# Switch-routed experts after local attention: experts' rows read as whole regions and turned in 32x32 blocks

## The chip, the cores and the metric

One core of a Trainium2 chip runs the whole program. The metric is the device time of one execution in microseconds, the median over several runs. The engines are named as in the profile: PE (TensorE, matrix products), DVE (VectorE), ACT (ScalarE), POOL (GpSimd) and SP, which issues most transfers.

## What is computed

An attention block with 4 batches, 8 heads, 768 positions and heads of 64, and behind it a layer of 8 experts, of which each token takes one. Cut from the reference:

```python
scores = scale * q @ k.T                      # per batch and head
keep = is_global | is_local                   # the first 8 keys, and the last 96 up to the query
scores = where(keep, scores - slope[h] * dist, -1e9)
a = softmax(scores);  attn = a @ v
x = attn.transpose(0, 2, 1, 3).reshape(3072, 512)
logits = x @ w_gate                           # 512 x 8
expert_idx = argmax(logits); gate_w = softmax(logits)[expert_idx]
for e in range(8):
    xe = x[expert_idx == e]
    out[expert_idx == e] = gate_w * (relu(xe @ w1[e]) @ w2[e])   # 512 x 1024, 1024 x 512
```

All data is float32.

## The kernel before

The program is recorded as one list of operations (`Flow`), and each engine runs its own operations in the order of that list; waits are derived from what each operation reads and writes. So the place of a line in the list is its place in its engine's queue, and an operation that waits holds up whatever stands behind it on the same engine. A transfer belongs to the queue of the engine that issues it: SP for plain loads, POOL for gathers and scatters.

**Attention** runs in 24 steps of 128 tokens (`steps(n)`, six per batch). A step computes the scores of its own block against itself and the block before (L456), adds the distance terms on DVE (`weigh`, L466, in two halves), takes the exponential on ACT (L474), sums on POOL (`both`, L480), and multiplies with the values of the step before (`values_part`, L493). It also finishes older blocks: `sums` and `tokens_x` (L508, L515) transpose the finished output, `tokens_u` (L518) the small sums, `normal` (L527 to L531) makes logits, `rows` (L536) writes the token's row. `k_in` (L432) and `q_in` (L440) transpose the keys and queries of two steps ahead. `k_in` uses a PSUM bank that the second half of `weigh` reads; `tokens_x` writes the bank that `rows` reads. POOL copies the global keys and values over the first rows of a block (L980, L1025). SP issues the loads of q and k four steps ahead, of v three steps ahead, and from step 5 on one piece of expert 0's weights per step.

**Routing.** After every sixth block `choose` finds each token's expert, `counts` ranks the tokens with small products on PE, `slots` turns ranks into row numbers, and six `scatter` calls per batch write rows of 516 words (512 of x, the gate, the token's number) into a table in device memory, xg_dram, where every expert has a region of its own. The ninth region (E, "late") takes expert 0's tokens of the last batch, so that expert 0 can start on the first three batches. `tables` and `all_counts` make the lists by which rows are gathered, the masks of unused rows, and the index of the size form of each group.

**Experts** run in the order 0, E, 1 to 7. `gather` (L702, on POOL) reads a group's rows, 128 per call. `x_in` transposes them on PE, four 128x128 transposes per 128 rows (L725), and ACT evicts them (L727). The two products of an expert are each done with seven products of quarter matrices instead of eight (`seven`): `up` twice seven steps (steps 0 to 13), `down` seven (steps 14 to 20; D is 14). All products stand in L758. Sums of quarters come from DVE: `x_sums` (L732 to L735), `w_sums` (L662 to L665, 128x1024 elements each), `h_sums` (L819 to L822), and inside the steps the additions that evict PSUM (L784, L795, L799, L804, L809); ACT copies the first product of each seven out (L780). `at_(i, ...)` hangs other work behind step i. `y_out` transposes the results back (L741), scales them by the gate (L744) and scatters them to the output (L747, POOL). `marks` copies the gates and makes the output row numbers from the gathered rows. `w_pieces(e)` are the eight weight transfers of an expert, 512 KB each, on SP. Group E uses plain products (`plain`).

At a boundary between two experts the order before is:

```python
ex.marks(g)
for j in (1, 3, 0, 2):
    ex.x_in(g, j)
if nxt is not None and g != E:
    ex.gather(nxt, [])
for fn in ex.x_sums():
    fn()
```

and then the first two up steps with the results of the group before between them.

## Time and profile before

| | |
|---|---|
| three runs | 572.89 us median, 572.22 to 573.99 |
| the profiled execution | 570.95 us, of which the span from first to last instruction is 569.2 |
| PE busy | 502.5 us, 88% of the span |
| DVE, ACT, POOL busy | 333.4 us (59%), 193.2 us (34%), 175.6 us (31%) |
| mean granted PE clock | 0.964 |
| the quarter products (L758) | 314.8 us of PE |
| transposes of x (L725) and of y (L741) | 19.4 us and 18.8 us of PE, 136 each |
| moved by DMA | 72.76 MB, mean 128 GB/s |

How to read it: a group of instructions is named by its line, engine and operation. The clock row gives, for each fortieth of the span, the share of full speed that PE was granted. A list of waits names for each engine what ended its idle time. In a timeline row the columns are the start and length in us, the engine (PEld are weight loads, an engine with a q at its end is its queue), the line, the operation, what it writes and reads, how many instructions the row covers, and in brackets the idle time before it and what ended that. Ends of matmuls are modelled.

### The profile page before, as it was taken

To read this page: it belongs to the slowest core of one execution; us is meant where nothing else is said; L and a number is where in the kernel's file an instruction comes from. 1 tells how busy PE (TensorE), PEld (TensorE's weight loads), DVE (VectorE), ACT (ScalarE), POOL (GpSimd) and SP (SyncE) were. 2 spreads that over 40 slices of the span, in tenths; PEclk is the share of its full clock that TensorE was granted. 3 is DMA by queue.
4 is the path that set the end of the run, shared out by engine and by line. 5 is a ranking of instruction groups with operands and counts; after the bars stand their busy time and mean duration, and the time that the engine had idled before them with its cause. 6 is when DMAs were issued, how large, how long until landed. Compare 5 with 4: busy or idle time off the path is not lost.

```text
span 569.2 us, 11005 instructions
## 1 busy us (share of the span) xinstructions
PE 502.5 (88%) x4537; PEld 468.8 (82%) x4537; DVE 333.4 (59%) x596; ACT 193.2 (34%) x325; POOL 175.6 (31%) x205
## 2 busy tenths in 40 slices
PE   4999899898774979989999999999999999999940
PEld 4888788787654879979998998999999998998940
DVE  5465855887762662716674674665774664666520
ACT  3666465566232220332223223223223213205200
POOL 2654475676454044322005014005005005003020
PEclk9999999999796989989999999999999999999995
DMA  8978787574152055371443433443443433001010
GB/s 180 216 190 213 202 218 202 137 185 122 40 170 85 1 184 190 126 260 33 149 150 119 149 150 106 149 150 118 149 150 112 149 116 134 1 1 60 1 40 7
DMA packets 97547, 72.76 MB, mean 128 GB/s; under 512 B 80568, under 2 KB 80568, under 8 KB 97472
## 3 DMA queue, kind: packets, MB, share of 16 engines
q1 hardware_dynamic: 89280, 52.70, 31.9%
q0 software_dynamic: 7360, 18.99, 9.8%
q8 instruction: 54, 0.88, 0.6%
q14 instruction: 21, 0.17, 0.1%
q10 hardware_dynamic: 832, 0.02, 0.1%
HBM read 61.69 MB, written 15.25 MB: 135 GB/s over the span
## 4 chain that ended last, share of the span: by engine, by line
PE 75%; DVE 11%; issue 4%; ACT 3%; POOL 2%; DMA 2%; POOLq 0%; ACTq 0%; DVEq 0%; SPq 0%
PE psum L758 50%; PE psum L456 6%; PE psum L493 5%; DVE arena L466 4%; PE psum L741 3%; PE psum L432 2%; PE psum L508 2%; PE psum L725 2%; PE psum L440 2%; PE psum L515 2%; ACT arena L727 2%; DVE arena L822 1%; DMA xg_dram<-arena,slot_i 1%; DVE arena L784 1%; DMA words<-in_n_local_dram 1%
## 5 line engine op out<-in xcount | busy, mean ns | idle before, releaser
L758 PE MATMUL psum<-arena 128*128 128x208 f32 (+6 forms) x1920 | 314.8, 325 | 9.6 <-DVE arena L784 5.5
L758 PEld LDWEIGHTS psum<-arena 128*128 128x128 f32 x1920 | 303.3, 191 | 17.1 <-DVE arena L784 7.6
L702 POOL DMA_INDIRECT arena<-xg_dram,grow x34 | 37.1, 1092 | 204.9 <-DVE arena L732 169.2
L466 DVE TENSOR_TENSOR arena<-psum,arena 128x1024 f32<-128x1024 f32 x40 | 48.7, 1220 | 39.1 <-PE psum L456 39.1
L480 POOL TENSOR_TENSOR arena<-arena 128x512 f32<-128x512 f32 x40 | 54.0, 1350 | 36.5 <-ACT arena L474 36.4
L474 ACT ACTIVATE arena<-arena 128x1024 f32<-128x1024 f32 (+1 forms) x48 | 47.4, 987 | 52.5 <-DVE arena L466 48.5
L747 POOL DMA_INDIRECT out_dram<-arena,to x34 | 35.4, 1040 | 75.2 <-ACT arena L744 39.7
L776 ACT ACTIVATE arena<-arena 128x512 f32<-128x512 f32 x48 | 30.2, 630 | 76.7 <-DVE arena L799 41.4
L493 PE MATMUL psum<-arena 128*64 128x128 f32 x704 | 45.6, 282 | 7.7 <-POOL arena L1025 6.6
L456 PE MATMUL psum<-arena 64*128 64x128 f32 x704 | 48.5, 288 | 1.4 <-ACT arena L434 0.7
L493 PEld LDWEIGHTS psum<-arena 128*64 128x64 f32 x704 | 39.3, 140 | 11.1 <-POOL arena L1025 7.0
L456 PEld LDWEIGHTS psum<-arena 64*128 64x128 f32 x704 | 43.6, 196 | 5.5 <-issue 3.2
L727 ACT COPY arena<-psum 128x512 f32<-128x512 f32 x34 | 18.5, 588 | 78.9 <-PE psum L725 78.9
L795 DVE TENSOR_TENSOR arena<-arena,psum 128x512 f32<-128x512 f32 x24 | 16.5, 688 | 45.8 <-PE psum L758 40.4
L588 POOL DMA_INDIRECT xg_dram<-arena,slot_i x24 | 24.1, 1002 | 28.4 <-DVE grow L687 23.5
L784 DVE TENSOR_TENSOR arena<-arena,psum 128x512 f32<-128x512 f32 x24 | 16.5, 686 | 27.6 <-PE psum L758 27.6
L432 PE MATMUL psum<-ident,arena 128*128 128x128 f32 x96 | 16.9, 303 | 15.3 <-DVE arena L466 8.6
L809 DVE TENSOR_TENSOR arena<-arena,psum 128x512 f32<-128x512 f32 x24 | 16.5, 688 | 21.9 <-PE psum L758 20.4
L799 DVE TENSOR_TENSOR arena<-arena,psum 128x512 f32<-128x512 f32 x24 | 16.5, 687 | 19.1 <-PE psum L758 17.1
L432 PEld LDWEIGHTS psum<-ident,arena 128*128 128x128 f32 x96 | 11.1, 151 | 19.9 <-issue 13.2
L804 DVE TENSOR_TENSOR arena<-arena,psum 128x512 f32<-128x512 f32 x24 | 16.5, 688 | 16.0 <-PE psum L758 13.4
L744 ACT ACTIVATE arena<-psum,gate 128x512 f32<-128x512 f32 x32 | 20.4, 684 | 11.0 <-PE psum L741 10.8
(137 smaller groups left out, 516.2 us busy)
## 6 DMA issues: line engine op xcount, KB each, us to landing
arena<-in_moe_w_dram SPq DMA_DIRECT2D x64, 512.0 KB, 4.3
arena<-in_q_dram SPq DMA_DIRECT2D x24, 256.0 KB, 3.9
arena<-in_k_dram SPq DMA_DIRECT2D x24, 256.0 KB, 4.6
arena<-in_v_dram SPq DMA_DIRECT2D x24, 256.0 KB, 5.1
arena<-xg_dram,grow POOLq DMA_INDIRECT x34
out_dram<-arena,to POOLq DMA_INDIRECT x34
xg_dram<-arena,slot_i POOLq DMA_INDIRECT x24
arena<-in_v_dram SPq DMA_DIRECT2D x4, 64.0 KB, 3.5
```

The source lines that it names most:

```text
L432: f.pe.transpose(pt[:, m, :], raw[:, 2 * m:2 * m + 2, :].rearrange("p a d -> p (a d)"), self.keep["ident"][:])
L456: f.pe.matmul(self.psum[:, 2 * g + a, c:c + P], lhsT=kt[r, m, :], rhs=qt[r, m, :], start=True, stop=True, skip_group_check=True)
L466: f.dve.tensor_tensor(e, s, self.bias[:, g, :, 1:3, :].rearrange("p h k c -> p h (k c)"), ALU.add)
L474: f.act.activation(e, e, AF.Exp)
L480: f.pool.tensor_tensor(self.es[n % 3][:, g], e[:, :, 0:P], e[:, :, P:2 * P], ALU.add)
L493: f.pe.matmul(po[r, m, :], lhsT=self.v[(n - ab) % 6][:, 2 * m + a, :], rhs=self.e[n % 2][:, m // 2, 2 * a + m % 2, P * ab:P * ab + P], sta ...
L588: self.f.pool.indirect_dma_start(out=self.xs[:], out_offset=bass.IndirectOffsetOnAxis(ap=k["slot_i"][:, b % 2, u:u + 1], axis=0), in_=self ...
L702: self.f.pool.indirect_dma_start(out=self.x[g][:, j, :].bitcast(I32), out_offset=None, in_=self.xs[:], in_offset=bass.IndirectOffsetOnAxis ...
L727: f.act.copy(self.xt[:, :, hh, ts(bb, 128)], pt)
L747: f.pool.indirect_dma_start(out=self.out[:], out_offset=bass.IndirectOffsetOnAxis(ap=k["to"][:, g, j:j + 1], axis=0), in_=self.y[j], in_of ...
L758: f.pe.matmul(self.psum[:, bank, 256 * t:256 * t + 256], lhsT=w[k][:, ts(t, 128)], rhs=x[k], start=(fresh and t == 0 and k == 0), stop=Tru ...
L776: f.act.activation(d, d, act)
```

## The change

- The gathers are gone. `load_x` reads a group's region as a whole with plain transfers on SP: four per half of the rows, each of 32 partitions x 8 runs of 512 bytes, and one or two small ones of 8 bytes per row for gate and token number (into `gt`). They are laid out so that a transpose within blocks of 32x32 gives the layout that the products read.
- `x_in` is now two DVE block transposes per expert (one for E), 128x1024 elements each, without PE, PSUM and ACT. To fit the order of channels that this gives, the w1 pieces take their rows in another order: 4 blocks of 32 rows for each piece.
- Rows of a region that no token fills have to be zero. `blank` writes zeros over the regions of 0, 1 and E after step 1 of attention (SP, 1280 rows of 2064 bytes); `pads` scatters zeros to the unused rows of experts 2 to 7 (POOL, four calls per expert), by `pad_table`.
- For experts 1 to 7 the first two of each four `w_sums` are on POOL.
- The order is new: in a step, `counts` one step later, `slots` behind the second half of `weigh`, `q_in` ahead of `k_in` and both behind `tokens_x`; the last batch's six scatters of step 21 in one go; the routing of the last batch spread over steps 2 to 14 of group 0; x work of the next expert at the down steps; `h_sums` spread over steps 7 to 13 instead of behind steps 6 and 13.

The core of the diff:

```diff
+    def gates(self, b):          # split off from choose()
+        f, k, V = self.f, self.keep, self.f.dve
...
-        x, xl = a(4, self.XW), a(2, self.XW)
+        x, xl = a(2, 8, 4, 32), a(1, 8, 4, 32)
...
+        s = self.moe_w1[e].rearrange("(q c d) f -> c q d f", q=4, d=32)
+        for c in range(4):
+            out.append(lambda d=w["w1"][:, c, :], s=s[c]: f.sp.dma_start(out=d, in_=s))
...
-        return [lambda: V.tensor_tensor(c["t3"], c["b22"], c["b12"], ALU.subtract),
-                lambda: V.tensor_tensor(c["t1"], c["b12"], c["b11"], ALU.subtract),
+        first = self.f.pool if e else V
+        return [lambda: first.tensor_tensor(c["t3"], c["b22"], c["b12"], ALU.subtract),
+                lambda: first.tensor_tensor(c["t1"], c["b12"], c["b11"], ALU.subtract),
...
+    def load_x(self, g, tokens):
+        f, k = self.f, self.keep
+        late = g == self.E
+        nh = 1 if late else 2
+        rows = self.xs[g * self.REGION:g * self.REGION + 256 * nh, :]
+        for hh in range(nh):
+            for qd in range(4):
+                src = rows[:, ts(qd, 128)].rearrange("(b t h) d -> h t b d", t=32, h=nh)[hh]
+                f.sp.dma_start(out=self.x[g][32 * qd:32 * qd + 32, hh].rearrange("p b c d -> p b (c d)").bitcast(I32),
+                               in_=src, _r=list(tokens))
...
-    def x_in(self, g, j, bank=None):
-        f = self.f
-        pt = self.bank() if bank is None else self.psum[:, bank, :].rearrange("p (c t) -> p c t", c=4)
-        for c in range(4):
-            f.pe.transpose(pt[:, c, :], self.x[g][:, j, ts(c, 128)], self.keep["ident"][:])
-        hh, bb = (j % 2, j // 2) if g != self.E else (0, j)
-        f.act.copy(self.xt[:, :, hh, ts(bb, 128)], pt)
+    def x_in(self, g, hh):
+        self.f.dve.transpose(out=self.xt[:, :, hh, :].rearrange("p c (b t) -> p b c t", t=32),
+                             in_=self.x[g][:, hh])
...
-            if n == N - 1:
-                ex.gather(0, sum(tokens[:B - 1], []))
...
-                kk = at.k_in(n + 2, SK)
             if n >= 2:
                 at.tokens_x(n - 2, T0)
             if n + 2 < N:
                 qq = at.q_in(n + 2, T1)
+                kk = at.k_in(n + 2, SK)
...
+                f.pool.memset(ex.zero, 0.0)
+                for g in (0, 1, E):
+                    ex.blank(g)
...
-            for _ in range(3 if b == B - 1 and i >= 3 else 1):
+            for _ in range(NBLK if b == B - 1 and i >= 3 else 1):
                 if scat:
                     at.scatter(*scat.pop(0))
+            if n == N - 3:
+                ex.load_x(0, sum(tokens[:B - 1], []))
...
+                if nxt is not None and g != E:
+                    ex.load_x(nxt, [f"pad{nxt}.{j}" for j in range(4)])
...
+                h0, h1 = ex.h_sums(0), ex.h_sums(1)
+                for i, fn in zip((7, 8, 9, 11), h0):
+                    at_(i, fn)
+                at_(13, *h1)
...
+                    last = sum(tokens, [])
+                    ex.load_x(E, last)
+                    for fn in pieces[:4]:
+                        fn()
+                    ex.load_x(1, last)
+                at_(2, lambda: at.normal(N - 1, U), lambda: at.choose(B - 1), *pieces[4:])
+                at_(4, lambda: at.counts(U), lambda: at.gates(B - 1))
+                at_(5, lambda: at.slots(B - 1, U))
+                at_(6, lambda: at.rows(N - 1, T0), scatters)
...
+                at_(0, sums[0], sums[1], sums[4], sums[5])      # group E: POOL's four for expert 1
+                at_(2, sums[2])
+                at_(3, sums[3], lambda: ex.x_in(1, 0))
+                at_(4, lambda: ex.x_in(1, 1), *xs, *pieces[:4])
...
+                    at_(6, sums[0], sums[1])                    # the other groups
+                    at_(11, sums[4], sums[5])
+                    at_(D, lambda: ex.x_in(nxt, 0), lambda: ex.x_in(nxt, 1))
+                    at_(D + 1, sums[2])
+                    at_(D + 2, sums[3], xs[0])
+                    at_(D + 3, sums[6], xs[1])
+                    at_(D + 4, xs[2])
+                    at_(D + 5, xs[3], sums[7])
+                    at_(D + 6, lambda: ex.marks(nxt))
+                    at_(3, lambda: ex.pads(after))
```

## The prediction

> **What bounds the kernel now.** I read the page's parts 1 and 2 first, then TensorE's list of waits, then the chain, and then the timeline around the gaps. The profiled execution took 570.95 us: a span of 569.2 and 1.75 outside it. That is 1.9 below the median of the three runs (572.89), so I add 1.9 to the sum at the end.
>
> ```profile
> PE 502.5 (88%) x4537; PEld 468.8 (82%) x4537; DVE 333.4 (59%) x596; ACT 193.2 (34%) x325; POOL 175.6 (31%) x205
> PEclk9999999999796989989999999999999999999995
> ```
>
> TensorE is busy 88% of the span and the bound nearly everywhere, so what counts is work taken off it and gaps closed. The clock row falls where the gaps are. Waits of TensorE, in us, times and longest:
>
> ```profile
> PE psum L432 <- DVE arena L466: 8.6, 7, 3.3
> PE psum L493 <- POOL arena L1025: 6.6, 1, 6.6
> PE psum L758 <- DVE arena L784: 5.5, 6, 3.1
> PE psum L725 <- issue: 2.6, 1, 2.6
> PE psum L566 <- DVE oh L553: 2.1, 3, 0.7
> ```
>
> A boundary between two experts, in the timeline:
>
> ```profile
> 293.23 1.04 PE L725 MATMUL psum<-ident,arena 128*128 128x128 f32 x8
> 294.60 1.12 PE L725 MATMUL psum<-ident,arena 128*128 128x128 f32 x8 [0.33 <-ACT arena L727]
> 295.99 1.06 PE L741 MATMUL psum<-ident,arena 128*128 128x128 f32 x8 [0.28 <-ACT arena L727]
> ```
>
> The x transposes (L725) hold TensorE from 293.23 to 295.99: 2.76 us per expert, eviction waits included. The end of attention:
>
> ```profile
> 170.29 1.04 POOL L702 DMA_INDIRECT arena<-xg_dram,grow  x1 [4.31 <-DMA xg_dram<-arena,slot_i]
> 177.14 3.25 PE L493 MATMUL psum<-arena 128*64 128x128 f32 x28 [6.61 <-POOL arena L1025]
> 177.41 0.93 DVE L712 COPY gate<-arena 128x4 f32<-128x4 f32 x1 [6.97 <-DMA arena<-xg_dram,grow]
> ```
>
> POOL stands in its queue for the scatters, then issues four gathers, and the copy that TensorE needs is behind them.
>
> **The change, part by part** (minus is a gain).
>
> *Boundaries between experts.* The 16 transposes per boundary go: -2.76. The h sums leave the place where L784 waited behind them (0.48 in this group; the 0.98 before it waits for ScalarE's L780 and stays): -3.24 together. VectorE gets two block transposes of 1024 elements instead. No row shows one; 1024 elements cost 1.22 in L466, 512 cost 0.69, so I take 1.2 each (0.6 to 2.4). [...] They stand at the first down step, which lasts 2.5 us (seven in 17.7). Behind them waits the u2 addition, wanted two steps later, so at 1.2 they are covered, at 2.4 they stall about 1.
>
> Half the weight differences move to POOL. L480 takes 1.27 us for 512 elements, so 2.5 for 1024, four per expert. These meet VectorE:
>
> ```profile
> 115.62 0.60 POOL L1025 COPY arena<-arena 32x512 f32<-32x512 f32 x1
> 115.74 1.57 DVE L663 TENSOR_TENSOR arena<-arena 128x1024 f32<-128x1024 f32 x1
> 116.41 2.02 POOL L480 TENSOR_TENSOR arena<-arena 128x512 f32<-128x512 f32 x1 [0.19 <-ACT arena L474]
> ```
>
> A sum of VectorE with both inputs in SBUF takes 1.57 instead of 1.22 beside a POOL copy, and POOL's next takes 2.02 instead of 1.27: each waits until the other has finished. POOL reaches its four sums after four output scatters and four pad scatters of 1.3, about 14 us into a group, and is then busy to 24. The h sums now stand at up steps 7 to 13, about 13 to 22 us in. The second would wait 0.85, the third up to 2.45, the additions queue behind them, and a step has 1.25 to spare: 3.3 - 1.25 = 2.1. The last four wait again and hold the second down step 1.2. So 0 to 3.4 per group; I take 1.6. Six boundaries are concerned.
>
> *Loads.* Each expert's x is now ten transfers on SP (0.37 to 0.58 each to issue, as L340), issued a whole up phase (21 us) before use, and landing took 2.9 to 6.3: covered. Ahead of them on SP is only the wait for the pads of a group earlier; behind them the next w1, which waits for TensorE anyway. Without that cover an x transfer costs its length, some 8 us (5.5 of issues and 2.9 of landing). Pads replace gathers on POOL one for one: in the path only by moving POOL's sums 5 us later, as reckoned above. But w1 pieces now come from a source list of 4 blocks of 32 rows instead of 128 rows. Window 285 to 299 moved 149 GB/s at a DMA share of 0.43, so 347 at full share: 2 MB take 6.0 us. No row shows how a list led by a count of 4 is shared out; at a quarter of the engines it would be 24. I take 0.3 per boundary (0 to 2). [...]
>
> So -3.24 + 1.6 + 0.3 = -1.3 per boundary, six times: **-8** (-20 to +10).
>
> *Attention steps 3 to 20.* k_in now follows tokens_x. This row shows the price:
>
> ```profile
> 36.59 0.68 DVE L536 TENSOR_TENSOR arena<-psum,small 128x512 f32<-128x512 f32 x1
> 36.91 0.66 PE L432 MATMUL psum<-ident,arena 128*128 128x128 f32 x4
> 37.40 0.60 PE L515 MATMUL psum<-ident,arena 128*128 128x128 f32 x4
> ```
>
> tokens_x (L515) overwrites the bank that L536 reads until 37.27; today k_in fills TensorE from 36.91 meanwhile. With tokens_x first TensorE waits 0.4. Ten plain steps: **+4** (0 to +7). At steps 8/9 and 14/15 the removed wait of 0.69 on oh and 1.43 on L466 come back, because the weights' addition, slots and rows are the same VectorE chain: 0. The blank writes (1280 rows of 2064 bytes, 2.6 MB, 7.6 us at 347 GB/s) stand on SP ahead of step 6's loads, which have 16 us and take 4.2; with w1 of expert 0: **+1** (0 to +6).
>
> *Step 21 to the first product of group 0*: now 142.56 to 184.50, 41.9 us. After, from step 21's start: weights' addition ends 4.8, slots 6.4, POOL is free of its own sums at 7.2; six scatters of 1.3 end at 14.8; landing 4.3 (as at 170.29): 19.1; ten issues 5.5; landing about 2.9: 27.5; marks 0.3 and the first block transpose 1.2: 29.1. marks(0) waits on VectorE for the last of these transfers; queued behind it are the normalizing and rows of step 22, which TensorE needs only after its first product. TensorE alone would be ready at 25. The 3.35 gap at 147, the 6.61 gap and the slow clock after both go: **-12.8** (-15 to -8; if the scatters land in 8.5, as they do after 209, it is -8.6).
>
> *Group 0*: now 184.5 to 228.0. Gone: the 3.07 wait for L784 behind slots and tables, 0.86 on L799, some 1.4 of slow clock, 1.2 of E's transposes; added: 0.8 before step 1, where tokens_x waits for x work and rows on VectorE. With VectorE's queue followed step by step I get 38.4: **-5** (-7 to -2). Scatters start 13.5 in instead of 17. The counts, choices and tables moved between steps are the same 25 or so instructions of 0.15 to 0.9; VectorE hides them as long as it is not a step behind, and today's 3.07 is what they cost uncovered.
>
> *Group E to expert 1*: transposes 248.17 to 251.37 go (-3.2), the 2.63 gap may stay; but w1 of expert 1 now stands on SP behind the scatters and E's x, POOL's sums and VectorE's behind that: **-2** (-5 to +6). *Last group*: **-0.5**.
>
> Sum: -8 + 4 + 1 - 12.8 - 5 - 2 - 0.5 = -23.3. 569.2 - 23.3 + 1.75 = 547.6; with 1.9 to the median, **549.5 us**.
>
> **Rivals.**
> 1. *Clean*: POOL and VectorE miss each other. Boundaries -3.24 x 6 = -19.4 instead of -8: -35, 538. For: VectorE has gaps of 1 to 2 us between additions. Against: 115.74 above.
> 2. *Contention in full*: 3.4 per group leaves boundaries at about +0.5 x 6 = +3: -12, 561. For it: POOL got its turn between two of VectorE's sums at 297.48 (1.50 instead of 1.0).
> 3. *Slower: loads become the bound.* Place: the engines that carry w1. Per expert: w1, plus w2 6, x about 5 (512-byte pieces), output and pads 5. It decides when w1 takes over 26 us, so that loads exceed today's 42.4 per group (293.23 to 335.64). At w1 = 30, groups last 46: +3.6 x 6 = +21.6, attention +10, E +8, against -12.8 - 5: +22, 595 us. Against: w1 taken at a quarter of 347 GB/s is 24.
>
> **How the numbers follow.** Forecast 0.5, rival 1 0.2, rival 2 0.17, rival 3 0.1, no measurable change 0.03. The range reaches over rivals 1 and 2 with their unknowns and leaves out rival 3: 533 to 568. 0.3% (1.7 us) is about what a measurement of this kernel can tell from no change. Faster 0.86, same 0.03, slower 0.11.
>
> **What would show it.** In the changed profile: no 128x128 transposes of x on TensorE; a block transpose of about 1.2 us, two per expert; TensorE waiting some 0.4 for L536 before tokens_x; the first product of group 0 near 177; group periods of 39 to 42 us instead of 42.4; h sums above 0.69 us beside POOL's 2.5. The prediction is wrong if TensorE's waits in the groups end in a w1 or x transfer, if the block transpose takes over 2 us, or if the POOL sums last far above 2.5.

## The result, and the profile after

The changed kernel takes **594.96 us** (median of 4 runs, 591.3 to 596.4), the kernel before in runs beside it 572.93 (572.22 to 573.99): ratio 1.0373, 95% interval 1.0322 to 1.0425. It is slower by 22 us; the forecast was 23 us faster, and the range (533 to 568) does not hold it. Rival 3 does, though not by all of its mechanism; that it meets the time to the microsecond is chance. The profiled execution took 596.4 us with a span of 594.2. All stages below are from spans: 569.2 before, 594.2 after. Ratios in this document leave out executions that took over 1.5% longer than the shortest of the same kernel, which are six of the ten of `e1` and one of the ten of `e4`.

First the page of the changed kernel, lines of parts 1, 2 and 3:

```profile
PE 498.3 (84%) x4401; PEld 467.1 (79%) x4401; DVE 336.0 (57%) x585; ACT 174.7 (29%) x291; POOL 230.0 (39%) x223
PEclk9999989999889999779999998997998997998995
DMA  9995589987152434485393292286177158001010
q1 hardware_dynamic: 113344, 64.29, 45.5%
q8 instruction: 54, 0.88, 0.7%
```

TensorE has lost only 4.2 of its 502.5 busy us: the 136 transposes are gone (19.4), but a slower clock gives much of it back (the same 1920 quarter products take 326.4 us instead of 314.8; the mean clock is 0.939, it was 0.964). The clock row now has a dip in nearly every group. The plain transfers hold the DMA engines 45.5% of the span. The last line is one to remember: instructions, the engines' code, are listed there among what the 16 DMA engines carry, as a queue of their own (54 packets of 16 KB, 0.7% of the span).

TensorE's waits, in us, times and longest:

```profile
PE psum L801 <- issue: 24.8, 7, 5.5
PE psum L801 <- DVE arena L769: 14.4, 1, 14.4
PE psum L432 <- DMA arena<-in_k_dram: 8.1, 3, 7.2
PE psum L515 <- DVE arena L536: 7.9, 15, 1.2
PE psum L801 <- DVE arena L838: 4.8, 5, 1.5
PE psum L440 <- DMA arena<-in_q_dram: 3.5, 1, 3.5
```

Two of these did not exist before (2.6 us of "issue" at L725 and 0.6 at L758 aside): 24.8 us in which this list names nothing that TensorE waits for, in seven gaps, and one wait of 14.4 for the block transpose. Of the 8.1 on k, 7.2 is the first load of the program, which stood before as 6.7 on L359. Where the 25.0 us of span went, stage by stage (first product of an expert, or first transpose of its results, as marks):

| stage | before | after | difference | forecast |
|---|---|---|---|---|
| start of attention to step 21 | 142.6 | 153.5 | +10.9 | +5 |
| step 21 to group 0's first product | 41.9 | 31.8 | -10.1 | -12.8 |
| group 0 | 43.5 | 37.5 | -6.0 | -5 |
| group E to expert 1's first product | 24.7 | 31.8 | +7.1 | -2 |
| expert 1, to its boundary | 43.3 | 48.1 | +4.8 | } -8 |
| the five groups behind it | 218.2 | 236.2 | +17.9 | } |
| the last group and the end | 55.0 | 55.4 | +0.4 | -0.5 |

The transition from group E to expert 1, in the timeline of the changed kernel (rows of SP, POOL, DVE and PE):

```profile
211.15 4.89 SPq L653 DMA_DIRECT2D arena<-in_moe_w_dram  x4
216.09 24.70 SPq L743 DMA_DIRECT2D arena<-xg_dram  x8
241.97 2.33 POOL L674 TENSOR_TENSOR arena<-arena 128x1024 f32<-128x1024 f32 x1 [12.18 <-DMA arena<-in_moe_w_dram]
246.76 3.35 DVE L676 TENSOR_TENSOR arena<-arena 128x1024 f32<-128x1024 f32 x1 [23.05 <-POOL arena L675]
253.30 2.36 DVE L769 STREAM_TRANSPOSE arena<-arena 128x1024 f32<-128x1024 f32 x2
254.59 1.65 PE L801 MATMUL psum<-arena 128*128 128x256 f32 x3 [14.44 <-DVE arena L769]
```

w1 of expert 1 is issued at 211.15 and POOL may use it at 241.97: 2 MB in 30.8 us, where the prediction took 6. SP takes 24.7 us to issue eight x transfers of 128 KB (3.8 in `e9`). POOL's sums, VectorE's, the block transpose and TensorE stand behind each other. The releaser in TensorE's wait (L769) is the last link, the cause is four links up.

A boundary between two experts:

```profile
303.58 1.89 PE L801 MATMUL psum<-arena 128*128 128x256 f32 x8
305.31 1.04 PE L784 MATMUL psum<-ident,arena 128*128 128x128 f32 x8
310.73 1.58 PE L801 MATMUL psum<-arena 128*128 128x184 f32 x4 [4.39 <-issue]
308.00:310.00 2.00, 0.00 (x0) 0.00 (x0) 0.00 (x0) 0.00 (x0) 1.43 (x2) 1.00 0.94 317
```

Each group's products stand in the program in several versions for different numbers of tokens (its *forms*); TensorE goes to the one that fits by a branch. The first product in the form (128x184) comes 4.39 us after TensorE has finished all that stands ahead of it. The last row is from the windows (PE, PEld, DVE, ACT and POOL busy, granted clock, DMA share, GB/s): all engines but POOL stand still, and the DMA engines are at 0.94.

### The profile page after: what moved, and what is told of

Same layout as the page of the kernel before. It is cut to its first block, busy times and chain, and to the rows that moved or that the text cites. A ratio compares the mean times of both kernels' runs of the same rounds, so it can differ in the third digit from the quotient of the medians.

```text
span 594.2 us, 10750 instructions
## 1 busy us (share of the span) xinstructions
PE 498.3 (84%) x4401; PEld 467.1 (79%) x4401; DVE 336.0 (57%) x585; ACT 174.7 (29%) x291; POOL 230.0 (39%) x223
## 3 DMA queue, kind: packets, MB, share of 16 engines
q1 hardware_dynamic: 113344, 64.29, 45.5%
## 4 chain that ended last, share of the span: by engine, by line
PE 60%; DVE 15%; DMA 10%; issue 8%; ACT 2%; POOL 2%; SPq 1%; POOLq 0%; DVEq 0%; ACTq 0%
PE psum L801 43%; DVE arena L466 6%; DMA arena<-in_moe_w_dram 5%; DMA arena<-in_k_dram 5%; PE psum L456 4%; PE psum L493 2%; PE psum L515 2%; PE psum L784 2%; PE psum L432 2%; PE psum L440 2%; PE psum L508 1%; DVE arena L864 1%; DVE arena L536 1%; DVE arena L863 1%; DVE arena L862 1%
## 5 line engine op out<-in xcount | busy, mean ns | idle before, releaser
L801 PE MATMUL psum<-arena 128*128 128x208 f32 (+6 forms) x1920 | 326.4, 333 | 44.9 <-issue 24.8
L801 PEld LDWEIGHTS psum<-arena 128*128 128x128 f32 x1920 | 314.9, 197 | 52.1 <-issue 26.4
L466 DVE TENSOR_TENSOR arena<-psum,arena 128x1024 f32<-128x1024 f32 x40 | 48.8, 1220 | 49.7 <-PE psum L456 38.1
L474 ACT ACTIVATE arena<-arena 128x1024 f32<-128x1024 f32 (+1 forms) x48 | 47.4, 987 | 45.5 <-DVE arena L466 39.8
L838 DVE TENSOR_TENSOR arena<-arena,psum 128x512 f32<-128x512 f32 x24 | 16.4, 685 | 71.6 <-PE psum L801 53.7
L493 PE MATMUL psum<-arena 128*64 128x128 f32 x704 | 44.0, 277 | 1.1 <-issue 1.1
L823 ACT COPY arena<-psum 128x512 f32<-128x512 f32 x24 | 14.0, 582 | 100.2 <-PE psum L801 100.2
L493 PEld LDWEIGHTS psum<-arena 128*64 128x64 f32 x704 | 38.3, 138 | 4.2 <-issue 1.5
L674 POOL TENSOR_TENSOR arena<-arena 128x1024 f32<-128x1024 f32 x14 | 34.0, 2426 | 17.5 <-DMA arena<-in_moe_w_dram 17.5
L675 POOL TENSOR_TENSOR arena<-arena 128x1024 f32<-128x1024 f32 x14 | 35.6, 2541 | 1.1
L592 POOL DMA_INDIRECT xg_dram<-arena,slot_i x24 | 27.1, 1129 | 21.8 <-DVE arena L852 16.3
L676 DVE TENSOR_TENSOR arena<-arena 128x1024 f32<-128x1024 f32 x16 | 21.9, 1371 | 23.0 <-POOL arena L675 23.0
L827 DVE TENSOR_TENSOR arena<-arena,psum 128x512 f32<-128x512 f32 x24 | 16.4, 682 | 30.0 <-PE psum L801 29.3
L787 ACT ACTIVATE arena<-psum,gt 128x512 f32<-128x512 f32 x32 | 20.3, 683 | 27.1 <-PE psum L784 27.1
L720 POOL DMA_INDIRECT xg_dram<-small,pad x24 | 23.3, 972 | 11.4 <-issue 6.7
L832 ACT ACTIVATE arena<-psum 128x512 f32<-128x512 f32 x16 | 9.6, 597 | 54.8 <-PE psum L801 31.0
L847 DVE TENSOR_TENSOR arena<-arena,psum 128x512 f32<-128x512 f32 x24 | 16.5, 687 | 14.7 <-PE psum L801 14.6
```

Of the source, the lines that this page charges most:

```text
L466: f.dve.tensor_tensor(e, s, self.bias[:, g, :, 1:3, :].rearrange("p h k c -> p h (k c)"), ALU.add)
L474: f.act.activation(e, e, AF.Exp)
L493: f.pe.matmul(po[r, m, :], lhsT=self.v[(n - ab) % 6][:, 2 * m + a, :], rhs=self.e[n % 2][:, m // 2, 2 * a + m % 2, P * ab:P * ab + P], sta ...
L592: self.f.pool.indirect_dma_start(out=self.xs[:], out_offset=bass.IndirectOffsetOnAxis(ap=k["slot_i"][:, b % 2, u:u + 1], axis=0), in_=self ...
L674: return [lambda: first.tensor_tensor(c["t3"], c["b22"], c["b12"], ALU.subtract), lambda: first.tensor_tensor(c["t1"], c["b12"], c["b11"], ...
L675: lambda: first.tensor_tensor(c["t1"], c["b12"], c["b11"], ALU.subtract),
```

## The experiments

Each run has its own comparison with the kernel before on the same chip; ratios are given with their 95% intervals, and a difference of two ratios is turned into us with 573. Four theories are named in the expectations: **A**, the w1 source list led by a count of 4 is carried by few DMA engines; **B**, the new order itself; **C**, the code that TensorE goes on with stands behind packets; **L**, the code needs a fixed time after the hint, which the removed transposes used to cover. The hint is an instruction that the program gives TensorE some work ahead of the branch; it names the form that will be chosen.

### The order of w1's source

`e1`: the same layout and bytes, but each transfer fills 32 partitions with 4 rows each.

```diff
-        s = self.moe_w1[e].rearrange("(q c d) f -> c q d f", q=4, d=32)
-        for c in range(4):
-            out.append(lambda d=w["w1"][:, c, :], s=s[c]: f.sp.dma_start(out=d, in_=s))
+        s = self.moe_w1[e].rearrange("(q c d) f -> q d c f", q=4, d=32)
+        for q in range(4):
+            out.append(lambda d=w["w1"][32 * q:32 * q + 32, :, :], s=s[q]: f.sp.dma_start(out=d, in_=s))
```

> The changed kernel, but each of the four w1 transfers of an expert fills 32 partitions with 4 rows each, so that its list of sources is led by a count of 32 instead of 4; the same 512 KB each, the same layout in the end. Theory A (a list led by 4 is carried by a quarter of the engines, and w1's 2 MB then take some 30 us and fill those engines, so that everything else that shares them lands late): w1 of expert 1, issued at about 211, lands some 8 to 12 us later instead of 31; the 14.4 us wait for the block transpose ahead of expert 1 falls to 1 to 3; the waits of TensorE on k and q transfers (8.1 and 3.5) go; issues of x on SP take 4 us and not 14; groups last 40 to 43 instead of 45. In all 14.4 - 2 + 11.6 + 6 x 2 to 4 = 36 to 48 less than 595: 547 to 559. Rival B (the new order itself, POOL's sums beside VectorE's and x on the SP queue make the loss): less than 10 us are won, 585 to 595.

Measured: 1.0081 (1.0041 to 1.0122), so 1.0373 - 1.0081 = 2.9%, **17 us**. That is the upper end: the ten runs spread from 566.4 to 583.3 us, and by the mean of all ten the gain is 12. The wait of 14.4 has shrunk to 1.6, the k and q waits behind the program's first load are gone, and w1 of expert 1 lands 10.6 us (median of its four) after its issue instead of 31. But 17 is less than half of what theory A promised: the gaps of "issue" stayed, in new sizes (7.8 after group E, 4.2 behind it, 0.4 to 2.4 in the others; with runs that spread so far, these sizes of one execution are rough).

`e2`: the kernel before, and only its w1 transfers take the 4-led source (the first diff's removed lines).

> The kernel before, with nothing changed but the source order of its w1 transfers, which are led by a count of 4 as in the changed kernel (expert 1 and the others then get w1's rows in another order, so the output differs). Theory A: w1 takes 24 to 31 us instead of about 6 to 10; expert 0's pieces in attention have a step each and make the k and q loads late (some 10 us), in the groups the gathers and scatters wait behind w1's packets: 573 + 10 to 30 = 583 to 603. Rival B: 573, as before, and no transfer lands later.

Measured: 1.0072 (1.0047 to 1.0096), **4 us**. The weights' median landing goes from 4.3 to 14.3 us, and TensorE loses little: 9.1 instead of 6.6 for POOL's copy ahead of L493, 2.0 on k. How the list is carried can be read where w1 moves alone. The rows give the DMA share in tenths, in 40 slices: first the kernel before from 275 to 285, then `e2` from 270 to 280, and the share of the plain transfers there:

```profile
DMA  8799997999820000000000000000000000000000
DMA  2222222222222222132022223320332213226222
q1 hardware_dynamic: 336, 0.87, 25.2%
```

With the 4-led list the share stays at a quarter of the 16 engines, without a break. In the changed kernel w1 moves at the same share, 0.25 to 0.27, and 102 to 109 GB/s (231 to 235, 328 to 340), where 347 was reckoned; from 328 to 332 four packets are under way at a time in 91% of the stretch, of 4 KB and 159 ns each, where the kernel before has 16 or more, of the same size and time, in 94% of 240 to 244. This is theory A's mechanism. The slow list costs 4 us where w1 has a whole group (42 us) to land, and 12 to 17 where w1 stands behind the scatters, and SP's next transfers behind w1.

### Which engine makes the weight differences, and the order in attention

`e3`: `e1`, and `first = V` in `w_sums` (no sums on POOL). `e4`: `e1`, and `k_in` ahead of `tokens_x`, evicted ahead of `q_in`, as before the change.

```diff
-        first = self.f.pool if e else V
+        first = V                                        # e3
+            if n + 2 < N:                                # e4
+                kk = at.k_in(n + 2, SK)
             if n >= 2:
                 at.tokens_x(n - 2, T0)
             if n + 2 < N:
                 qq = at.q_in(n + 2, T1)
-                kk = at.k_in(n + 2, SK)
```

> As the kernel with w1 led by 32, and all weight differences are on VectorE, none on POOL. If POOL's sums and VectorE's hold each other up as the prediction took it (1.6 us per boundary, 0 to 3.4), six boundaries: 0 to 20 us less than the kernel with w1 led by 32, most likely 5 to 10. The rival: VectorE has no room for four more sums of 1.2 us in a group, and TensorE waits for its additions: 0 to 10 us more.

> As the kernel with w1 led by 32, and in attention the keys of two steps ahead are again transposed ahead of the token block, and evicted ahead of the queries, as before the change. By the prediction's 0.4 per step for ten plain steps: 4 us less than the kernel with w1 led by 32 (0 to 7). The rival: the wait that the old order had on VectorE's adding of the distance terms (8.6 us over seven waits) comes back and eats it: 0, or up to 4 us more.

Measured: `e3` 0.9963 (0.9931 to 0.9994), 6.8 us under `e1`: 1.1 per boundary, where the prediction took 1.6. `e4` 0.991 (0.9875 to 0.9945), 9.8 us under `e1`: more than the 0 to 7 of the prediction. (Against the mean of all runs of `e1` they are 12 and 14, so 1.1 is the lower end.) In `e4` the waits on L536 are 0.3, and group 0's first product is at 169.2, in `e3`, with the attention of the change, at 177.3: 8.1 us. The wait of L432 on L466 comes back with 1.7 only, not with the 8.6 it had.

### The gaps with no releaser

`e5`: `e4`, and x is issued at the first down step, ahead of the next w1, instead of at the boundary. `e6`: `e4`, and 16 transposes of the identity behind each hint.

```diff
-                    at_(D, *pieces[:4])                                      # e5
+                    at_(D, lambda: ex.load_x(after, [f"pad{after}.{j}" for j in range(4)]), *pieces[:4])
                 f.hint(*forms[g])                                            # e6
+                for bank in (ex.bank(), ex.bank()):
+                    for c in range(8):
+                        f.pe.transpose(bank[:, c % 4, :], keep["ident"][:], keep["ident"][:])
```

> As the kernel with w1 led by 32 and the keys first, and the x of the next expert is issued on SP one group phase earlier: at the first down step, ahead of the next w1, instead of at the boundary behind the last weights. What it tests is the gap that TensorE shows between experts with nothing to wait for (issue: 23.4 us over seven gaps, 8.3 after group E, 5.3 in one of the others). Theory C (the code that TensorE goes on with is fetched behind the packets of x): the 8.3 falls to about the 2.6 of the kernel before, the others from 1.3 to 5.3 to 0 to 1: 8 to 14 us less than with x at the boundary. Theory L (TensorE needs some 8 us after the hint in any case, and the removed transposes have shortened the work that lay between): the gaps stay, 0 to 2 us less.

> As the kernel with w1 led by 32 and the keys first, and behind the hint at each of the eight boundaries TensorE does 16 transposes of the identity that nobody reads, 2.0 us each time. Theory L (a fixed time from the hint to the chosen form): the gaps of 1.3 to 5.3 shrink by 2.0 and the time is the same to 4 us more. Theory C (the gap is the x packets' doing) gives the same where the gap is longer than 2.0 and the full 2.0 where it is shorter: 5 to 9 more. If the gaps have nothing to do with the hint: 2.0 x 8 = 16 more.

Measured: `e5` 0.999 (0.996 to 1.002), 4.6 us *over* `e4`: the narrow form of theory C, that x's packets alone do it, fell. The timeline and the windows of `e5` say why:

```profile
316.18 5.93 SPq L656 DMA_DIRECT2D arena<-in_moe_w_dram  x4
331.88 4.31 PE L801 MATMUL psum<-arena 128*128 128x200 f32 x14 [4.97 <-issue]
326.00:328.00 2.00, 0.91 (x9) 0.67 (x7) 0.69 (x1) 1.27 (x2) 1.43 (x2) 1.00 1.02 358
330.00:332.00 2.00, 0.12 (x1) 0.14 (x2) 0.00 (x0) 0.00 (x0) 1.39 (x3) 1.00 1.03 399
332.00:334.00 2.00, 2.00 (x7) 2.00 (x8) 0.00 (x0) 0.00 (x0) 1.70 (x2) 0.51 0.61 220
```

x, w1 and w2 now stand in one row, from 308.8 to 333, across the boundary. The DMA share is 1.0 until 332, TensorE starts when it falls, and has half its clock for the next 2 us. That suggests a wider form of theory C: whatever is queued there, x or weights, holds the code. `e9` and `e13` test it.

`e6` gave 1.0112 (1.0079 to 1.0145), 11.6 us over `e4` for 16 us of work. The gaps at L801 shrank from 23.4 to 2.7 (8.5 moved ahead of the first of the new transposes), but the waits on L838 and L842 rose from 8.8 to 22.9. The time is not the 0 to 4 that theory L wanted, but the run does not decide: the gaps did shrink, and the additional waits are another cause.

`e8`: the kernel before without its x transposes from expert 1 on. It prices the first term of the prediction.

```diff
                     ex.marks(g)
-                    for j in (1, 3, 0, 2):
-                        ex.x_in(g, j)
```

> The kernel before without the x transposes and their evictions at the boundaries, in all groups from expert 1 on (these experts then compute with rows that are left of group E). Gathers, sums, weights stay. It prices the first term of the prediction: 2.76 us of TensorE per boundary, 3.37 after group E. If the term is right: 6 x 2.76 + 3.37 = 20 us less, 546 to 548 where before takes 566.5. Theory L (a fixed time from the hint to the form's code, which the transposes cover): waits of TensorE with no releaser appear at each boundary, 1 to 3 us each, and the gain is 3 to 12 us.

Measured: 0.9904 (0.9872 to 0.9935), **5.5 us** of the 20. The timeline shows who takes their place:

```profile
341.23 1.99 PE L758 MATMUL psum<-arena 128*128 128x256 f32 x8 [1.17 <-DVE arena L733]
344.96 3.30 PE L758 MATMUL psum<-arena 128*128 128x200 f32 x18 [1.74 <-issue]
```

Of the 14.5 us that did not come, 7.4 are waits for VectorE's x sums (which the change does move away), 2.5 for ACT's copies (L780, 4.0 instead of 1.5), and some 4 are gaps with no releaser: 4.9 instead of 2.6 after group E, 1.9 instead of 0.6 at L758. The transposes were cover for all three. Since the change moves the x sums away, the term's worth to the change itself is nearer to 5.5 + 7.4 = 13 of the 20 (an estimate).

`e9`: `e4`, and x is issued when the form's first result is out, by letting its transfers read the first quarter of h.

```diff
-                if nxt is not None and g != E:                      # at the boundary
-                    ex.load_x(nxt, [f"pad{nxt}.{j}" for j in range(4)])
+                if nxt is not None:                                 # behind step 3 of the group
+                    at_(3, lambda: ex.load_x(nxt, [f"pad{nxt}.{j}" for j in range(4)] + [ex.h[:, 0:2, 0]]))
```

> As the kernel with w1 led by 32 and the keys first, and the x of the next expert is issued only when the first result of the chosen form is out (it waits for the first quarter of h that the form writes), so that no x packet is queued while TensorE goes over to the form. Theory C, in the wider form that the trace of the x-early kernel suggests (TensorE's code comes over the same DMA engines and stands behind whatever is queued there: there the DMA share was 1.0 from 320 to 332 and TensorE went on at 331.9): the gaps at the six boundaries behind expert 1 (1.3 to 5.3) fall under 0.5, with the slow clock behind them: 8 to 15 us less than that kernel, ratio to before 0.965 to 0.978. The gap of 8.3 after group E stays, since there w1 and w2 are queued. Theory L (a fixed time after the hint): the gaps stay, and x comes later: 0 to 4 us more.

Measured: **0.9768** (0.9701 to 0.9835), 8.1 us under `e4`. The waits of "issue" fall from 23.4 to 15.1, of which 7.6 is the gap after group E, where w1 and w2 are still queued; the gaps at the later boundaries are 0.2 to 2.1 instead of 1.3 to 5.3. Under 0.5, as expected, they are not.

`e11` and `e13` ask the same of the kernel before. In `e11` the w1 transfers stand at the last down step in the list (`at_(D + 6, *pieces)` for the two lines of before):

> The kernel before, with one thing changed: from expert 1 on an expert's four w1 transfers are issued at the last down step together with w2, not at the first, so that 4 MB and not 2 are queued when TensorE goes over to the next expert. They are wanted 20 us later, which leaves the weights themselves room. TensorE does the same work. Theory C: gaps with no releaser at the boundaries, 3 to 5 us each with a clock of 0.5 behind them, 5 boundaries: 15 to 30 us more, ratio 1.03 to 1.05. Theory L, or if the code comes another way: the time of before, 1.00.

Measured 1.0004 (0.9983 to 1.0026), but the run says nothing: SP goes through its queue by itself, w1 waits only for its buffer, and it went out as early as before: at the boundary stand only w2's four (issued from 328.17, in the kernel before from 330.22). The new place in the list alone moved no transfer of w1 here. `e13` gives w1 a wait, on top of that edit:

```diff
-                out.append(lambda d=dst[:, c:c + step, :], s=s[:, c:c + step, :]: f.sp.dma_start(out=d, in_=s))
+                out.append(lambda d=dst[:, c:c + step, :], s=s[:, c:c + step, :]: f.sp.dma_start(
+                    out=d, in_=s, _r=[self.yt[:, 2:4, 0]] if e > 2 else []))
```

> The kernel before, and from expert 3 on the four w1 transfers of an expert wait for the last result of the down phase (the last quarter of yt), so that w1 and w2, 4 MB and some 10 to 12 us of all DMA engines, are queued just when TensorE goes over to the next expert. They are wanted 20 us later. Theory C: gaps with no releaser of 2 to 6 us at five boundaries, with a clock near 0.5 behind them: 12 to 35 us more, ratio 1.02 to 1.06. If the code does not share the engines with the packets: 1.00, at most 3 us more for gathers that land later.

Measured: 1.0099 (1.0067 to 1.0131), **5.7 us**. This is the run in which nothing but the time of transfers changes, with w1 in its old order. The gaps appear: 8.6 us in five, here the longest.

```profile
PE psum L759 <- issue: 8.6, 5, 4.1
484.69 2.80 PE L759 MATMUL psum<-arena 128*128 128x200 f32 x11 [4.09 <-issue]
482.00:484.00 2.00, 0.00 (x0) 0.00 (x0) 0.00 (x0) 0.00 (x0) 1.39 (x3) 1.00 1.05 395
486.00:488.00 2.00, 2.00 (x8) 1.99 (x7) 0.00 (x0) 0.60 (x1) 0.98 (x2) 0.50 1.08 395
```

So theory C holds in kind: packets at the boundary make gaps on a kernel that has its transposes. In size it was under what was expected (12 to 35 us): four of the five gaps are 0.8 to 1.3.

The traces can say more than the list of waits, for they hold TensorE's branch to the form (L250), the hint (L230) and every DMA packet. One boundary each of the kernel before, the changed one and `e13`, the branch's length in ns and its start in us:

```profile
L250 PEldq COMPARE_BRANCH  x1: 1091/1091/1091, 298.5 to 298.5; - x1
L250 PEldq COMPARE_BRANCH  x1: 5583/5583/5583, 305.0 to 305.0; - x1
L250 PEldq COMPARE_BRANCH  x1: 6669/6669/6669, 477.9 to 477.9; - x1
```

The branch holds TensorE's queue, and it ends 1.3 to 1.5 us after the end of a 16 KB packet of q8, at each of the six boundaries behind expert 1 in these three kernels. So the gaps are the wait for code. The packet itself takes 0.9 to 1.7 us; what moves is its start: 5.1 to 5.6 us after the hint in the kernel before (7.4 once), 6.5 to 9.6 in the changed kernel, 7.7 to 11.4 where `e13` queues its weights, 9.0 to 11.6 in `e5`, and 4.7 to 6.2 at the first five boundaries of `e9`. That is theory C. Theory L is not quite out: at the last boundary, where few or no packets are queued, the branch still ends 7.9 us after the hint in the kernel before (DMA share 0.01), 9.0 in the changed one (0.14, with a gap of 2.2), and 5.9 in `e9` (0.02, no gap). So there is a delay without packets too, though not a fixed one. The transposes covered it: the branch stands 6.5 to 6.9 us behind the hint before, 5.3 to 5.6 after. In four of the five boundaries of `e13` it ends 10.0 to 11.1 us after the hint, hardly earlier than in the changed kernel (10.0 to 12.4 where the DMA share is above 0.9); the gaps are shorter there, and TensorE has the 2.8 us of transposes in front of them.

### The two fixes, and the sums again

`e10`: `e9`, and w1 and w2 of expert 2 issued in expert 1's group. `e7` is `e5`, `e12` is `e10`, `e14` is `e9`, each with all differences on VectorE (`first = V`, as in `e3`).

```diff
-                at_(4, lambda: ex.x_in(1, 1), *xs, *pieces[:4])              # e10, group E
-                at_(5, sums[6], sums[7], lambda: ex.marks(1), *pieces[4:])
+                at_(4, lambda: ex.x_in(1, 1), *xs)
+                at_(5, sums[6], sums[7], lambda: ex.marks(1))
                     at_(2, check)                                            # expert 1
+                    at_(4, *ex.w_pieces(2))
```

> As the kernel with x after the code, and expert 2's w1 and w2 are issued in expert 1's group, behind x, instead of during group E. Theory C: the gap of 8.3 after group E falls to 0 to 2.6 with the half clock behind it: 6 to 10 us less. The rival: the weights of expert 2 then land 12 us later and POOL's sums of them hold VectorE up: 0 to 4 more.

> As the kernel with x issued early, and all weight differences on VectorE. With w1 led by 32 alone this gave 6.7 us less (ratios 1.0081 and 0.9963), from TensorE's waits for VectorE's additions of 14.4 falling to 5.5. Here those waits are 8.8 to begin with: 3 to 7 us less, if the two edits add up; the rival is that VectorE, with 62% busy, becomes late at the first down steps, where x is turned: 0 to 3 more.

> As the kernel with x and the second weights after the code, and all weight differences on VectorE. With x early this edit cost 15 us (ratios 0.999 and 1.0268), with x at the boundary and the old attention order it won 6.7. By theory C that sign is the packets' doing: TensorE then runs 8 to 10 us faster into the boundary and meets more of them. Without packets at the boundary only VectorE's waits count: 8.8 us of waits on the additions become 5.5: 2 to 5 us less. The rival (VectorE late where x is turned): 5 to 15 more.

> As the kernel with x after the code (ratio 0.9768), and all weight differences on VectorE; the weights of expert 2 stay in group E. The same edit with expert 2's weights moved lost 6 us, of it 13.6 in one wait of VectorE for those weights. Theory: here that wait is gone and the waits on VectorE's additions fall from 9.7 to some 5.5: 3 to 6 us less, ratio 0.966 to 0.972. The rival (TensorE comes to the boundary earlier and meets w2's packets): gaps grow, 0.98 to 1.0.

Measured: `e10` 0.9778 (0.972 to 0.9837), `e7` 1.0268 (1.0239 to 1.0296), `e12` 0.9883 (0.986 to 0.9905), `e14` 0.9882 (0.9852 to 0.9911). In `e10` the gap after group E falls from 7.6 to 2.6, and that rest ends with VectorE's L776 (an x sum); the branch out of group E's form still takes 3.4 us there, with a DMA share of 0.02; it takes as long in the kernel before (3.44, with 0.68), and 8.5 in `e9`. TensorE waits 3.9 on L842 instead, and the time is the same. The sums on VectorE, which won 6.8 in `e3`, cost 16, 6 and 6.5 here. In `e7` the gaps of "issue" grow from 32.4 to 38.4. In `e12` the reason is one row: VectorE reaches the sums of a w1 that has not landed, and its queue stands.

```profile
256.71 1.23 DVE L674 TENSOR_TENSOR arena<-arena 128x1024 f32<-128x1024 f32 x1 [13.37 <-DMA arena<-in_moe_w_dram]
260.45 3.83 PE L801 MATMUL psum<-arena 128*128 128x208 f32 x10 [13.61 <-DVE arena L827]
248.00:252.00 4.00, 0.00 (x0) 0.00 (x0) 0.00 (x0) 0.00 (x0) 0.00 (x0) 0.61 1.02 210
256.00:260.00 4.00, 0.00 (x0) 0.00 (x0) 3.25 (x4) 0.00 (x0) 0.00 (x0) 0.50 1.05 388
```

With the sums on POOL (`e10`) the longest such wait of TensorE is 3.9. In `e14` TensorE instead stands inside the form, 3.15 us up to 300.67, behind a stretch with a DMA share of 1.05 to 1.26 (292 to 298). The two windows show one more thing: w1, filling 32 partitions per transfer, moves 210 GB/s with the engines fully taken, w2, with 128, 388. `e15`: `e14`, with w1 in 16 transfers of 32 rows, the four partition groups in turn. `e16`: `e15`, and expert 2's w2 (`w_pieces(2)[4:]`) in expert 1's group.

```diff
+        s = self.moe_w1[e].rearrange("(q c d) f -> c q d f", q=4, d=32)
+        for c in range(4):
+            out.append(lambda c=c, s=s[c]: [f.sp.dma_start(out=w["w1"][32 * q:32 * q + 32, c, :], in_=s[q])
+                                            for q in range(4)])
```

> As the kernel with x after the code and all differences on VectorE, and w1 in 16 transfers of 32 rows to 32 partitions, 128 KB each, the four partition groups in turn, instead of 4 transfers of 512 KB to one group each. If it is the one group of 32 partitions that halves the rate (205 against 388 GB/s), w1 now moves at 300 to 400 GB/s, frees the engines 4 us per expert, the gap of 7.6 after group E falls to 3 to 5: 2 to 6 us less. If the rate belongs to something else: the same time, or 1 to 3 more for 12 more issues of 0.45 on SP.

> As the kernel with w1 in 16 pieces, and expert 2's w2 (not its w1) is issued in expert 1's group behind x. Theory C: the gap after group E, with only w1 queued there, falls to 0 to 2.6: 3 to 6 us less than with w2 there, ratio 0.955 to 0.965. The rival: w2 lands late for the down sums of expert 2: up to 5 more.

Measured: `e15` 0.9757 (0.973 to 0.9784), 7 us under `e14`; `e16` 0.9766 (0.9721 to 0.9811), no difference. The gap after group E falls from 8.6 to 4.1, but w1 moves at only 221 to 270 GB/s and not at 300 to 400. Each piece still fills one group of 32 partitions, so the run does not tell the group from another cause, and why 16 pieces help by 7 us is not settled.

`e17`: `e9` with the 16 pieces. `e18`: `e15`, and x waits for a later result of the form.

```diff
-                    at_(3, lambda: ex.load_x(nxt, [f"pad{nxt}.{j}" for j in range(4)] + [ex.h[:, 0:2, 0]]))
+                    at_(4, lambda: ex.load_x(nxt, [f"pad{nxt}.{j}" for j in range(4)] + [ex.h[:, 4:6, 1]]))
```

> As the kernel with x after the code (POOL's sums, ratio 0.9768), and w1 in 16 pieces of 32 partitions in turn. On the kernel with VectorE's sums this edit won 7 us (ratios 0.9882 and 0.9757), since there VectorE waits for w1 itself. If w1's rate is what counts, 3 to 7 us less here too: 0.965 to 0.972. If it counted only where VectorE waits for w1: 0 to 2 less.

> As the kernel with w1 in 16 pieces and all differences on VectorE (0.9757), and x waits two more results of the form (the second quarter of h, some 3 us later). Theory C, inside the form too (the rest of the form's code stands behind x): TensorE's waits there (5.1 behind L824's copies, 3.3 and 2.7 behind additions) shrink by half, 3 to 8 us less: 0.962 to 0.971. If those waits are VectorE's own: 0 to 1 less, and x may land too late for the first down step, 2 to 6 more.

Measured: `e17` 0.9711 (0.9672 to 0.975), 3.3 under `e9`, with intervals that overlap; `e18` **0.961** (0.9579 to 0.964), 8.4 under `e15`: 543.97 us where before takes 565.94. It beats both kernels. In `e18` x goes out at 323.9, when the DMA engines are idle, and the waits inside the form behind L824 (5.1 in `e15`) and L843 (3.3) are gone. That it was the form's code that stood behind x there, as expected, is not shown: in `e14` no packet of q8 starts between 288.8 and 321.7, and the wait is at 300.67.

```profile
PE psum L802 <- issue: 8.8, 7, 3.2
PE psum L802 <- DVE arena L864: 3.3, 6, 1.0
PE psum L802 <- DVE arena L828: 3.2, 6, 0.8
323.00:325.00 2.00, 2.00 (x14) 2.00 (x13) 0.86 (x2) 1.14 (x2) 1.47 (x2) 1.00 0.08 4
323.93 4.08 SPq L744 DMA_DIRECT2D arena<-xg_dram  x8
```

## Why the prediction was wrong

**The step that failed** is the one under *Loads*: "No row shows how a list led by a count of 4 is shared out; at a quarter of the engines it would be 24. I take 0.3 per boundary (0 to 2)." The prediction had the right end of that range in hand and took the other. w1 held a quarter of the engines (`e2`, share 0.25): 2 MB took 30.8 us between groups 0 and 1, and at the 104 to 109 GB/s inside a group some 19 to 20 (an estimate). So w1 and the w2 behind it still fill the queue at the boundary. Undoing it gives back 12 to 17 us (`e1`). For the term of 0.3 per boundary the runs show 2.4: the five groups take 236.2 us in the changed kernel and 224.0 in `e4`, which has w1 led by 32 and otherwise only another order in attention (one execution each). The 24 of a quarter of the engines, which the prediction set beside this term, should have had the forecast over a rate read from w1 in another order: the share of 0.25 agrees with it.

**What was not in the sum at all:** the work behind the hint was cover. The first term, "the 16 transposes per boundary go: -2.76", took TensorE's time there as time on the path. `e8` paid 5.5 us for 20. What is late next, once the x sums are moved, is the form's code: late even with nearly idle DMA engines (2.2 us of gap at the last boundary, share 0.14), and later the longer they are taken. In the changed kernel, with x placed at the boundary and a slow w1, five of the gaps are 3.6 to 5.5 us. The forecast had priced x at the boundary as "covered", since x is wanted 21 us later; its price was in whom it delays. Moving it is worth 8.1 us (`e9`).

**Attention, +4 and +1:** +10.9. The +4 was mis-sized: 9.8 us by `e4`, 8.1 by its first product of group 0; the profile of the changed kernel shows 7.9 on L536 (15 waits of 0.35 to 1.17; taken 10 of 0.4). The "+1 (0 to +6)" for the first weights was 4.4 us of waits on q and k.

**Step 21 to group 0, -12.8:** -10.1, inside its range. **Group 0, -5:** -6.0. These held; with w1 led by 32 the first product is at 177.3 (`e3`), which is where the prediction put it.

**Contention, 1.6 per boundary:** the mechanism held: sums on POOL last 2.43 and 2.54 on average, and an h sum of VectorE took 2.83 beside one instead of 0.69 (from 322.92 to 325.76, where POOL's sum ends at 325.21; the additions of the same size with an input in PSUM stay at 0.69 or less beside POOL, 25 of them). By `e3` it is 1.1 to 1.9. But its sign depends on the loads: where w1 lands late, POOL is the better place to wait (`e14` takes 6.5 us more than `e9`).

**The block transpose:** 1.22 us on average over 17, as taken (1.2).

**Rival 3** said that w1 would decide above 26 us and that groups would then last 46; w1 took 31 once, and the five groups last 47.2 on average. Its sum (+21.6, +10, +8) is close to the stages (+22.7, +10.9, +7.1). But the groups are not long because the loads fill them, as it said: the DMA share over these five groups is 0.46. They are long because of where in the group the packets stand, for `e9` moves the same bytes at another time. With the keys first, x placed late, all sums on VectorE and w1 in small pieces (`e18`), the change is worth 22 us (0.961 of 573). That this is the size of the forecast is chance, since the forecast was for another kernel.

What stays open: why the code comes so late with no packets in its way (5.9 to 7.9 us after the hint at the last boundary; 3.4 us for the branch out of group E in `e10`), why 16 pieces help, and why x held the form up in `e15`.

## What to carry to other kernels

Before counting removed work as gained, ask what ran underneath it: here it was the fetch of the next code (`e8` was paid 5.5 us of 20), which the list of waits shows only as idle time with "issue" as its releaser; the branch's own record names it (5.58 us instead of 1.09 at one boundary). Look at the DMA share in the windows around a branch before placing a transfer there; a transfer whose data is wanted late was not free here when it was queued as TensorE went over to its next form (x moved away from there won 8.1 us in `e9`, w1 moved there cost 5.7 in `e13`), and a later place in the list did not hold it back (`e11`, 1.0004), a wait did (`e13`, 1.0099). When a change alters the order of a transfer's source, price the transfer at the few-engine end (here a share of 0.25, and 30.8 us for 2 MB) until a row shows otherwise.

## What the runs showed of the hardware

- Packets on the DMA engines delayed TensorE's code. The branch to a form ended 1.3 to 1.5 us after a 16 KB packet of the instruction queue, at six boundaries each of three kernels. That packet started 5.1 to 5.6 us after the hint in five of six boundaries of the kernel before, with a DMA share of 0.01 to 0.48 from the hint to the branch's end, and 9.0 to 11.6 in `e5`, with a DMA share of 0.95 to 1.04. At the last boundary, with a share of 0.01 and 0.02, the branch still ended 7.9 us after the hint in the kernel before and 5.9 in `e9`.
- Behind such a wait of 4.97 us (up to 331.88 in `e5`) and one of 4.09 (up to 484.69 in `e13`) TensorE had a clock of 0.5 for 2 us and of 0.63 and 0.66 for the next 2.
- Four transfers of 512 KB landed 30.8 us after their issue with a source led by 4, and 8.8 to 10.6 us (median of the four) with one led by 32. Led by 4 they held a quarter of the 16 engines (share 0.25 to 0.27).
- With the DMA engines at 1.0, transfers that fill 32 partitions moved 199 to 219 GB/s (from 265 to 271 us in `e9`), those that fill 128 moved 401 to 414 (from 240 to 244 us in the kernel before).
- A block transpose of 128x1024 float32 took 1.20 to 1.25 us on VectorE (17 of them in the changed kernel).
